# One bank and two written-out orders of a convolution and SiLU kernel on one core

## The chip, the cores and the metric

The kernel runs on one core of a Trainium2 chip. The metric is the device time of one execution in microseconds (us); the time before is the median of three runs. A separate profiled execution gives the trace.

## What is computed

```python
B, S, D = x.shape                       # 8, 4096, 192
w = softmax(weight, axis=-1)            # 8 heads x 7 taps
x_pad = zeros(6 rows) + x               # per sequence
out[b, s, h, g] = sum_k w[h, k] * x_pad[b, s + k, h, g]
h = out.reshape(32768, 192) @ w_in      # 192 x 2048
result = (h * sigmoid(h)) @ w_out       # 2048 x 192
```

A causal convolution of seven taps per head, then an up projection, SiLU, and a down projection, all in fp32.

## The kernel before, in words

**Blocks.** The 32,768 rows are cut into 32 blocks of 1,024 rows, each held as two halves of 512. Channels lie on partitions; 64 input channels are one contraction, so two products can lie on the two halves of the array's rows (`e` = 0 uses partitions 0 to 63, `e` = 1 partitions 64 to 127). From block 1 on both projections are computed with fewer multiplications, by sums of inputs and of weights.

**Up phase.** For five groups g of chunks (order `QUEUE`: 0, 4, 1, 2, 3) there are 15 products P*r*.*g* each (line 625), in three chains, each of which accumulates in a PSUM bank of its own: chain 1 is P5, P2, P6, P1, P0, P14, chain 2 is P3, P9, P7, P4, P8, chain 3 is P12, P10. Between two products of chain 1 ScalarE (ACT) copies the bank (tokens u5, u4, u2, u0, u1, line 674); between two of chain 2 VectorE (DVE) adds bank and copy (X2, X4 into the banks 5 and 6, then a5, a1, a0 into the hidden activations, line 668); after P12 and P10 VectorE subtracts bank 4 (b1, b5). P13 and P11 add to the banks 5 and 6. S0 to S5 are SiLU on ScalarE (line 686). `CHAIN_BANKS` names the bank of each chain and group; chain 3 has bank 4 in every group. One chunk is left plain: L.nk (line 642) is the product of half n with input part k. L.0k fills bank `PLAIN_BANKS[0]`; L.1k is two products of 256 columns, one on each half of the rows, into `PLAIN_BANKS[1]` and `PLAIN_BANKS[2]`. SL.0, SL.1 and SL.2 are their SiLUs (line 691).

**Down phase.** t.ji (line 709) are differences of hidden activations on VectorE. D*i*.*je* (line 741) are 48 groups of four products, 32 columns of the array each; i = 5 has 128 columns, the others 512. They add up in the banks `ACC` = 7, 1, 3, 5, 6, 4 for i = 0 to 5. z, y, x (lines 807, 804, 799) copy these banks on ScalarE, M1 to M7 (line 819) add them on VectorE, o transposes (line 829) and st stores them.

**Input of the next blocks.** ld loads two blocks ahead, i transposes on VectorE (line 464), ha sets the halo, v.ki is tap i of the convolution of part k (i = 0 on ScalarE, line 495, the rest on VectorE, line 498), sp spreads the result by DMA to both halves of the partitions (line 515), w makes sums of it (lines 532 and 535).

**The order.** Everything is issued in the order of two written-out lists of such tokens. `START` covers the first blocks (dp are the down products of block 0), `PLAN` is then run once per block; "-", "=" and "+" ahead of a token mean one block back, two back, one ahead. Engines work through their own instructions in that order, and `pin` keeps it. Each slot between two bars of `PLAN` holds one token of TensorE, so the list can be read as TensorE's order with the other engines' work beside it: "P12.1 | P6.2 u1.1 a5.1" puts u1.1 and a5.1 behind P6.2. Tiles and banks are reused, and a writer waits for the readers before it: P9 for X2, P10 for b1, P2 for u5, L.1k for whatever last read its banks.

```python
    QUEUE = (0, 4, 1, 2, 3)
    CHAIN_BANKS = ((0, 1, 7, 1, 0), (2, 3, 2, 3, 2), (4, 4, 4, 4, 4))
    CHAINS = ((5, 2, 6, 1, 0, 14), (3, 9, 7, 4, 8), (12, 10))
    ACC = (7, 1, 3, 5, 6, 4, 0)
    PLAIN_BANKS = (7, 7, 3)
    for b in range(3, NB + 2):
        for s in plan:
            for t in s:
                step(b, t)
```

Of the kernel before, what the change touches and what calls it, by code (L numbers as in the profile page):

```python
# [17 lines left out]
def kernel(  # L18
# [60 lines left out]


    PLAN = (
        "P5.0 | -P8.3 -S3.2 -sp.2 v.00 -t.01 | -D1.31 -S2.3 -S5.2 | -D1.01 -a0.2 -S1.3 =st.2 "
        "-a0.3 -S1.1 | -D1.11 -b5.3 -S0.2 | -D0.00 -S5.4 v.22 -sp.0 -S4.3 | -D2.01 -t.03 "
        "-S5.1 -S1.2 | -D0.20 =st.0 -t.02 -S0.3 | -D1.21 -S5.3 v.01 | -D2.00 v.11 | -D5.01 "
        "+ld.0 | -D0.30 v.02 | -D3.00 -t.10 | -D0.01 +ld.1 v.23 | -D0.31 v.24 | -D4.00 -t.11 "
        "+ld.2 | -D3.01 -w.0 | -D4.01 | -D0.11 -t.13 | -D2.11 -w.1 | -D5.00 | -D4.11 -t.12 | "
        "-D5.11 | -D2.10 -t.20 | -D4.10 -t.21 | -D5.10 | -D0.21 | -D0.10 -t.23 | -D3.11 "
        "-z1.0 v.25 u5.0 | -D4.20 v.03 | -D1.10 -t.22 | -D3.10 | -D4.21 -t.30 | -D1.20 v.12 "
        "| -D2.20 -t.31 | -D2.21 | -D1.30 -t.32 | -D3.21 -t.33 | -D5.20 | -D2.31 v.04 | "
        "-D1.00 v.26 | -D4.31 -w.2 | -D2.30 v.05 | -D5.30 -y2.0 | -D3.20 v.06 -y1.0 -M1.0 | "  # L90
        "-D3.31 v.13 | -D3.30 -M2.0 | -D5.31 v.14 -x0.0 | -D4.30 -y0.0 -M3.0 | -D5.21 -x1.0 "
        "| P2.0 | L.00 -M4.0 -x2.1 -w.3 | L.01 | P5.4 u4.0 -w.4 | L.02 | P6.0 u5.4 v.15 | "
        "P3.0 | P2.4 SL.0 v.16 u2.0 | L.12 -x2.3 X2.0 | L.11 -x2.2 u4.4 | L.10 -M5.0 | P9.0 "
        "| P1.0 +i.0 SL.2 SL.1 | P13.0 | P6.4 +i.1 -x2.0 u0.0 X4.0 | P3.4 | P5.1 u2.4 +i.2 "
        "S2.0 | P7.0 | P0.0 -M6.0 +ha.0 X2.4 | P12.0 | P11.0 u1.0 a5.0 u5.1 | P9.4 | P1.4 "
        "b1.0 S4.0 | P13.4 | P4.0 u0.4 X4.4 -w.5 | P10.0 | P2.1 a1.0 | P0.4 | P7.4 u4.1 b5.0 "
        "S2.4 | P11.4 | P8.0 -o.1 u1.4 a5.4 | P6.1 | P12.4 S4.4 a0.0 | P14.4 | P14.0 -M7.0 "
        "u2.1 S0.0 b1.4 | P4.4 | P3.1 S3.4 +v.10 | P10.4 | P1.1 X2.1 S3.0 a1.4 | P5.2 | P9.1 "
        "u0.1 | P0.1 | P13.1 u5.2 X4.1 | P2.2 b5.4 | P8.4 -o.3 | P7.1 | P5.3 u4.2 a0.4 -st.3 "
        "u1.1 | P6.2 | P12.1 S2.1 a5.1 u5.3 | P11.1 | P3.2 -st.1 b1.1 u2.2 S5.0 | P4.1 | "  # L100
        "P10.1 X2.2 S4.1 sp.1 | P2.3 S1.0 | P9.2 a1.1 -o.0 | P1.2 | P8.1 u4.3 X4.2 | P6.3 | "
        "P13.2 u0.2 a0.1 +v.20 | P11.2 b5.1 | P7.2 u2.3 -o.2 S2.2 | P0.2 | P3.3 S4.2 a5.2 | "
        "P1.3 | P12.2 u1.2 X2.3 | P4.2 u0.3 | P9.3 b1.2 S0.4 | P14.1 | P10.2 S1.4 X4.3 | "
        "P0.3 S3.1 | P7.3 b5.2 | P11.3 u1.3 a1.2 | P12.3 S0.1 a5.3 | P14.3 | P13.3 +v.21 | "
        "P4.3 S3.3 b1.3 | P8.2 a1.3 | P10.3 | P14.2 t.00"
    )
    START = (
        "=dp.37 =v.20 =v.00 =dp.19 =v.10 =dp.5 =dp.10 =dp.42 =dp.36 =dp.27 =dp.44 =dp.14 "
        "=dp.8 =dp.12 =dp.38 =dp.28 =dp.22 =dp.25 =dp.43 =dp.26 =dp.45 -ld.2 =dp.30 =dp.3 "
        "=dp.20 -ld.1 =dp.33 =dp.11 -ld.0 =dp.6 =v.01 =dp.17 =v.21 =dp.15 =v.02 =dp.18 =v.11 "  # L110
        "=v.03 =dp.16 =v.12 =dp.47 =v.04 =dp.0 =v.22 =v.13 =dp.23 =v.05 =dp.32 =v.14 =dp.34 "
        "=v.06 =dp.7 =v.15 =sp.0 =v.23 =dp.21 =v.16 =dp.4 =v.24 =sp.1 =dp.40 =v.25 =dp.39 "
        "=v.26 =go.2 =dp.31 -i.2 =sp.2 =dp.1 -i.1 -i.0 =dp.9 -ha.0 =dp.13 =dp.46 =dp.35 =w.0 "
        "-v.20 =dp.41 -v.10 =w.1 =dp.2 -v.11 =w.2 -L.01 -P5.0 -v.21 -L.00 -P5.4 -u5.0 =w.3 "
        "-L.02 -P2.0 -v.22 -v.12 =dp.24 -u4.0 -v.23 -v.00 =dp.29 -SL.0 =w.5 -u5.4 -P6.0 -P3.0 "
        "=cp.1 =cp.2 -P2.4 -u2.0 -X2.0 -L.12 -u4.4 -L.10 -v.01 =cp.0 -L.11 -P9.0 -P1.0 =o.0 "
        "-SL.2 -P13.0 -P6.4 -u0.0 -X4.0 -v.13 -P3.4 -P0.0 -u2.4 =w.4 -S2.0 -P12.0 -P11.0 "
        "-SL.1 -X2.4 -u1.0 -P7.0 -P5.1 -S4.0 -b1.0 -P9.4 -P1.4 -a5.0 -u5.1 -v.14 -P4.0 -P10.0 "
        "-u0.4 -X4.4 -P0.4 -a1.0 -v.15 -P2.1 -P7.4 -b5.0 -P8.0 -P11.4 -u4.1 -a5.4 -u1.4 -v.02 "
        "-P6.1 -P13.4 -a0.0 -P12.4 -P14.0 -u2.1 -v.03 -S2.4 -P3.1 -P1.1 -b1.4 -S3.0 -P4.4 "  # L120
        "-P14.4 -X2.1 -u0.1 -v.04 -P0.1 -P9.1 -S3.4 -a1.4 -S4.4 -P10.4 -P5.3 -X4.1 -P8.4 "
        "-v.16 -P5.2 -u5.3 -b5.4 -P7.1 -P2.3 -a0.4 -u5.2 -sp.1 -P12.1 -S5.0 -a5.1 -P2.2 -u1.1 "
        "-P13.1 -P4.1 -b1.1 -u4.2 -P3.2 =o.2 ld.2 -S2.1 -P6.2 -u4.3 -a1.1 -P10.1 -v.05 -P11.1 "
        "-u2.2 -P8.1 -X2.2 -P6.3 +ld.1 -S4.1 -v.24 -S0.4 -P9.2 -P1.2 -u2.3 -b5.1 -P14.1 "
        "-P13.2 -X4.2 -u0.2 ld.1 -a0.1 -P1.3 -P7.2 -S2.2 -v.25 -S3.1 -P0.2 -P3.3 -u0.3 -a5.2 "
        "-S1.0 =st.2 -P12.2 -P0.3 -X2.3 -u1.2 -P11.2 -P9.3 -b1.2 -u1.3 =st.0 -v.26 -P10.2 "
        "-P4.2 -S4.2 -X4.3 -P13.3 -P14.3 ld.0 -b5.2 -P14.2 -P7.3 -a1.2 -S2.3 -S1.4 -P12.3 "
        "-P11.3 -a5.3 -S0.0 -S3.3 -P4.3 -P8.2 -b1.3 -S0.1 =o.1 -S3.2 P5.0 -P10.3 -v.06 -S1.2 "
        "-D1.31 -t.00 u5.0 -sp.0 -S5.1 -D1.11 -a1.3 -D1.10 -t.01 =st.1 -D0.11 i.1 -sp.2 "
        "-D1.00 -a0.2 i.0 -S0.2 -D1.30 -t.03 -S5.2 -D0.00 -S4.3 -S1.3 -b5.3 -D2.00 -S1.1 "  # L130
# [12 lines left out]
        "a5.4 S4.4 P5.2 P3.1 b1.4 u2.1 P4.4 P10.4 u5.2 X2.1 v.16 P2.2 P9.1 a1.4 sp.1 P1.1 "
        "P13.1 u4.2 b5.4 X4.1 P8.4 P6.2 u0.1 +i.1 S1.0 P7.1 P0.1 a0.4 u2.2 S2.1 +i.0 P2.3 "
        "P12.1 u1.1 a5.1 +ha.0 P3.2 P1.2 b1.1 P4.1 u0.2 X2.2 P10.1 u4.3 P11.1 a1.1 P9.2 S0.4 "
        "-M7.0 P6.3 S4.1 P8.1 b5.1 P0.2 u2.3 P13.2 X4.2 +v.20 a0.1 P7.2 P11.2 u1.2 -o.0 S2.2 "
        "P3.3 P1.3 S0.1 a5.2 S4.2 P14.1 P12.2 X2.3 +v.10 u0.3 P9.3 P4.2 b1.2 P10.2 P0.3 X4.3 "
        "P11.3 P7.3 u1.3 b5.2 S0.0 a1.2 P12.3 P14.3 S5.0 a5.3 S1.4 P13.3 -o.2 S3.1 P4.3 b1.3 "
        "S3.3 P8.2 P14.2 a1.3 P10.3 t.00 +v.21"
    )  # L150
    QUEUE = (0, 4, 1, 2, 3)
    CHAIN_BANKS = ((0, 1, 7, 1, 0), (2, 3, 2, 3, 2), (4, 4, 4, 4, 4))

    def pin(ins):
        return tc.keep_in_program_order(ins)
# [37 lines left out]
    x0 = x.flatten_outer_dims()[TB - pad : TB, :].rearrange("t (k c) -> c k t", k=NK)  # L193
# [357 lines left out]
    def rows(t, e):  # L551
        return t[R * e : R * e + R]
# [46 lines left out]
    X_OF = {13: 0, 10: 5, 5: 3, 11: 4, 14: 1}  # L599
    CHAINS = ((5, 2, 6, 1, 0, 14), (3, 9, 7, 4, 8), (12, 10))  # L600
    ACC = (7, 1, 3, 5, 6, 4, 0)
    PLAIN_BANKS = (7, 7, 3)
    XBANK = {2: 5, 4: 6}

    def chain_bank(g, c):
        return banks[CHAIN_BANKS[c][QUEUE.index(g)]]

# [27 lines left out]
    def plain(b, n, k):  # L635
# [3 lines left out]
        for e in range(2) if n else (0,):  # L639
            cols = slice(e * TB // 2, (e + 1) * TB // 2) if n else slice(0, TB)  # L640
            pin(
                nc.tensor.matmul(  # L642
                    banks[PLAIN_BANKS[n and 1 + e]][:, cols],
                    rows(wr[j] if own == e else ws[j], e)[:, a, k, :],
# [7 lines left out]
    def h_of(b, g, o):  # L652
        a, j, e = PLAIN if g is None else chunks(g)[o // 2]
        return g_tile(b, j, a)[:, o % 2, e, :]
# [33 lines left out]
    def silu_plain(b, i):  # L688
        cols = slice((i - 1) * TB // 2, i * TB // 2) if i else slice(0, TB)
        h = h_of(b, None, int(i > 0))[:, cols]  # L690
        pin(nc.scalar.activation(h, banks[PLAIN_BANKS[i]][:, cols], AF.Silu))

# [418 lines left out]
```

## Time and profile before

| | |
|---|---|
| median of three runs | 2359.14 us (2359.13 to 2359.39) |
| profiled execution | 2359.21 us |
| its span, first to last instruction | 2357.4 us |
| granted TensorE clock | 0.999 |
| one block in the middle of the run, start of D to start of D | 72.38 us |
| DVE busy in the 36.10 us of its D phase | 32.86 us |
| DVE busy in the 36.20 us of its P phase | 32.68 us |
| ACT busy in the two phases | 9.39 us, 27.40 us |

The span is the time from the first to the last recorded instruction; the execution's own time has some 1.8 us around it. PE is TensorE's matmuls, PEld its weight loads, which run ahead of the matmuls and wait in their place. A row of the list of waits reads: who waited, for whom, in total us, how often, the longest. A matmul's end is modelled, so that two matmuls which follow each other with a short delay still count as one busy stretch.

### The profile page before, as it was taken

To read this page: it belongs to the slowest core of one execution; us is meant where nothing else is said; L and a number is where in the kernel's file an instruction comes from. 1 tells how busy PE (TensorE), PEld (TensorE's weight loads), DVE (VectorE), ACT (ScalarE), POOL (GpSimd) and SP (SyncE) were. 2 spreads that over 40 slices of the span, in tenths; PEclk is the share of its full clock that TensorE was granted. 3 is DMA by queue.
4 is the path that set the end of the run, shared out by engine and by line. 5 is a ranking of instruction groups with operands and counts; after the bars stand their busy time and mean duration, and the time that the engine had idled before them with its cause. 6 is when DMAs were issued, how large, how long until landed. Compare 5 with 4: busy or idle time off the path is not lost.

```text
span 2357.4 us, 43991 instructions
## 1 busy us (share of the span) xinstructions
PE 2349.2 (100%) x17630; PEld 1043.8 (44%) x17630; DVE 2110.6 (90%) x2877; ACT 1179.4 (50%) x2275; POOL 105.7 (4%) x168
## 2 busy tenths in 40 slices
PE   9999999999999999999999999999999999999998
PEld 4344443444444444444444444444444444444444
DVE  8999989899899999998998999999999989899867
ACT  5345644456544465444564445654446644456443
POOL 4910000000000000000000000000000000000000
PEclk9999999999999999999999999999999999999999
DMA  7232111222112221222221122212222112222111
GB/s 158 51 66 52 37 35 35 52 53 47 26 33 52 53 53 29 38 40 52 53 43 28 35 53 52 52 23 36 48 52 52 36 32 37 52 53 39 21 20 28
DMA packets 451245, 106.56 MB, mean 45 GB/s; under 512 B 423584, under 2 KB 428704, under 8 KB 451040
## 3 DMA queue, kind: packets, MB, share of 16 engines
q1 hardware_dynamic: 447392, 101.78, 23.7%
q8 instruction: 138, 2.26, 0.4%
q0 software_dynamic: 448, 1.58, 0.3%
q10 hardware_dynamic: 3200, 0.39, 0.1%
q14 instruction: 67, 0.55, 0.1%
HBM read 31.46 MB, written 25.17 MB: 24 GB/s over the span
## 4 chain that ended last, share of the span: by engine, by line
PE 99%; DVE 1%; ACT 0%; issue 0%; ACTq 0%; DVEq 0%
PE ps L741 47%; PE ps L625 45%; PE ps L642 2%; PE ps L762 2%; PE ps L570 2%; PE ps L1010 1%; PE ps L422 0%; DVE t L709 0%; DVE g L668 0%; DVE cmb L819 0%; DVE cmb L162 0%; ACT u L162 0%; ACT yx L804 0%; DVE osb L162 0%; DVE win L532 0%
## 5 line engine op out<-in xcount | busy, mean ns | idle before, releaser
L741 PE MATMUL ps<-g,wo 128*32 128x512 f32 x2976 | 691.9, 592 | 0.0
L625 PE MATMUL ps<-win,wr 64*128 64x512 f32 x1550 | 691.3, 595 | 0.0
L625 PE MATMUL ps<-win,ws 64*128 64x512 f32 x1550 | 674.3, 603 | 0.6 <-ACT u L674 0.6
L674 ACT COPY u<-ps 128x512 f32<-128x512 f32 x775 | 445.8, 589 | 184.6 <-PE ps L625 158.0
L741 PE MATMUL ps<-t,wo 128*32 128x512 f32 (+2 forms) x4528 | 536.6, 446 | 0.5 <-DVE t L709 0.5
L741 PE MATMUL ps<-t,wx 128*32 128x512 f32 x2976 | 495.7, 592 | 0.0
L625 PE MATMUL ps<-dup,wr 64*128 64x512 f32 x868 | 423.8, 590 | 0.0
L498 DVE SCALAR_TENSOR_TENSOR nat<-xt,taps,nat 128x512 f32<-128x512 f32 x564 | 415.4, 755 | 5.6 <-ACT nat L495 2.0
L709 DVE TENSOR_TENSOR t<-g 128x1024 f32<-128x1024 f32 x248 | 299.9, 1220 | 61.1 <-PE ps L741 41.0
L709 DVE TENSOR_TENSOR t<-g,t 128x1024 f32<-128x1024 f32 x248 | 302.7, 1221 | 30.0 <-PE ps L741 24.7
L625 PEld LDWEIGHTS ps<-win,wr 64*128 64x128 f32 x1550 | 261.4, 186 | 148.3 <-issue 62.4
L686 ACT ACTIVATE g<-ps 128x512 f32<-128x512 f32 x465 | 275.4, 602 | 83.8 <-PE ps L625 78.0
L668 DVE TENSOR_TENSOR g<-u,ps 128x512 f32<-128x512 f32 x465 | 305.7, 673 | 10.1 <-PE ps L625 1.4
L741 PEld LDWEIGHTS ps<-t,wo 128*32 128x32 f32 x4528 | 185.4, 110 | 274.2 <-issue 270.6
L625 PEld LDWEIGHTS ps<-win,ws 64*128 64x128 f32 x1550 | 242.6, 185 | 144.8 <-issue 49.5
L625 PE MATMUL ps<-dup,ws 64*128 64x512 f32 x682 | 280.9, 602 | 0.0
L668 DVE TENSOR_TENSOR ps<-u,ps 128x512 f32<-128x512 f32 x310 | 214.5, 692 | 69.8 <-PE ps L625 64.0
L686 ACT ACTIVATE g<-g 128x512 f32<-128x512 f32 x465 | 268.4, 633 | 15.3 <-DVE g L668 15.3
L804 ACT COPY yx<-ps 32x512 f32<-32x512 f32 x150 | 84.2, 579 | 380.0 <-PE ps L741 377.6
L741 PE MATMUL ps<-g,wx 128*32 128x512 f32 x1488 | 246.0, 594 | 0.0
L741 PEld LDWEIGHTS ps<-g,wo 128*32 128x32 f32 x2976 | 170.1, 110 | 112.5 <-issue 103.9
L807 ACT COPY cmb<-ps 96x512 f32<-96x512 f32 x30 | 17.5, 583 | 403.8 <-PE ps L741 403.8
(90 smaller groups left out, 1849.2 us busy)
## 6 DMA issues: line engine op xcount, KB each, us to landing
dup<-nat SPq DMA_DIRECT2D x345, 128.0 KB, 2.3
nat<-in_x_dram SPq DMA_DIRECT2D x382, 64.0 KB, 2.4
out_dram<-osb SPq DMA_DIRECT2D x376, 64.0 KB, 2.0
raw<-in_moe_w_out_dram SPq DMA_DIRECT2D x8, 384.0 KB, 3.6
raw<-in_moe_w_in_dram SPq DMA_DIRECT2D x12, 192.0 KB, 4.5
ws<-wr POOLq DMA_DIRECT2D x8, 192.0 KB, 5.0
raw<-in_moe_w_in_dram SPq DMA_DIRECT2D x6, 128.0 KB, 3.0
xt<-xt SPq DMA_DIRECT2D x31, 4.5 KB, 1.9
```

What stands on the lines that cost most here:

```text
L498: nc.vector.scalar_tensor_tensor(out=dst, in0=src, scalar=tap, in1=dst, op0=ALU.mult, op1=ALU.add)
L570: nc.tensor.matmul(hs[a, n, e], rows(wr[j], e)[:, a, k, :], rows(d, e)[:, n, k, :], start=k == 0, stop=k == NK - 1,)
L625: nc.tensor.matmul(to[:, cols], raw(g, *LEFT[e][r], e), rhs[:, cols], start=first, stop=True, skip_group_check=True,)
L642: nc.tensor.matmul(banks[PLAIN_BANKS[n and 1 + e]][:, cols], rows(wr[j] if own == e else ws[j], e)[:, a, k, :], rows(dups[b], e)[:, SLOT[e ...
L668: pin(nc.vector.tensor_tensor(out_, u, v, op=op))
L674: pin(nc.scalar.copy(us[b, g, o][:, cols], t1[:, cols]))
L686: pin(nc.scalar.activation(h, src, AF.Silu))
L709: pin(nc.vector.tensor_tensor(t[i // 2][:, i % 2, :], u, v, op=ALU.subtract))
L741: nc.tensor.matmul(accs[b][at][SQ * q : SQ * q + SQ, to], lhs[:, e, SQ * k : SQ * k + SQ], rhs[:, e, ts(q, TB // 4) if i == 5 else to], st ...
L762: nc.tensor.matmul(banks[DOWN_BANKS[k]][R * n : R * n + R, :], wo[j][:, a, e, R * k : R * k + R], gs[b, j, a][:, n, e, :], start=j == 0 an ...
L804: pin(nc.scalar.copy(to, acc[3 * (name[0] == "x") + k][n:P, :]))
L1010: nc.tensor.matmul(by_pe[k][n], rows(diag, n)[:, k, i, :], rows(xts[0], n)[:, k, i : i + TB], start=i == 0, stop=i == K - 1,)
```

## The change

`PLAIN_BANKS` goes from (7, 7, 3) to (7, 4, 3), and moves up beside the other tables: the first 256 columns of L.1k now lie in bank 4, which is that of chain 3, instead of bank 7, which holds L.0k. Both lists are written anew with the same tokens. Of the tokens of `PLAN`, nine have another block sign, since they stand at the other end of the list now (v.00, v.21, sp.0, st.0, st.2, a0.2, S0.1, S1.1, S5.1). In the diff, lines that are only "..." mark what is left out; the new `PLAN` is whole.

```diff
     PLAN = (
-        "P5.0 | -P8.3 -S3.2 -sp.2 v.00 -t.01 | -D1.31 -S2.3 -S5.2 | -D1.01 -a0.2 -S1.3 =st.2 "
...
-        "S2.0 | P7.0 | P0.0 -M6.0 +ha.0 X2.4 | P12.0 | P11.0 u1.0 a5.0 u5.1 | P9.4 | P1.4 "
-        "b1.0 S4.0 | P13.4 | P4.0 u0.4 X4.4 -w.5 | P10.0 | P2.1 a1.0 | P0.4 | P7.4 u4.1 b5.0 "
...
-        "P0.3 S3.1 | P7.3 b5.2 | P11.3 u1.3 a1.2 | P12.3 S0.1 a5.3 | P14.3 | P13.3 +v.21 | "
-        "P4.3 S3.3 b1.3 | P8.2 a1.3 | P10.3 | P14.2 t.00"
+        "P5.0 | -P8.3 -S0.1 -t.01 -S3.2 | -D0.11 -S5.2 v.01 -S2.3 | -D0.10 -a0.3 -S1.3 +ld.0 "
+        "-t.02 | -D1.20 -S0.3 -S5.4 | -D2.00 -S1.2 -t.03 -S4.3 | -D0.00 +ld.1 v.21 | -D2.01 "
+        "-b5.3 | -D1.21 v.22 -S5.3 -sp.2 | -D4.01 -S0.2 -t.10 | -D1.01 -t.11 | -D4.00 | "
+        "-D3.01 -t.12 | -D3.00 -t.13 +ld.2 | -D5.00 | -D2.11 -w.0 | -D5.01 | -D0.01 v.11 | "
+        "-D0.30 -t.20 | -D4.11 v.12 | -D4.10 v.02 | -D5.10 | -D2.10 -t.21 | -D3.10 -t.23 | "
+        "-D1.10 | -D5.11 v.13 | -D1.11 -w.1 | -D5.20 | -D1.00 v.03 | -D3.11 v.23 | -D1.30 "
+        "v.04 -t.22 | -D0.31 | -D4.21 -t.30 | -D1.31 -w.2 | -D0.20 v.14 | -D4.20 -t.31 | "
+        "-D2.21 | -D2.20 | -D5.21 -t.33 | -D2.31 | -D3.20 -t.32 | -D0.21 v.15 | -D5.30 -z1.0 "
+        "| -D2.30 v.05 | -D5.31 -M1.0 | -D3.31 -x2.2 v.24 -y2.0 | -D3.21 -x2.3 -w.3 u5.0 | "
+        "-D4.31 -x2.0 v.06 | -D3.30 v.25 | -D4.30 -w.5 -x0.0 -y1.0 -M2.0 | P3.0 | P2.0 -y0.0 "
+        "-M3.0 -x2.1 | P5.4 | L.01 -w.4 u4.0 -M4.0 | L.11 u5.4 +i.0 | P6.0 | L.00 -x1.0 v.16 "
+        "| L.10 u2.0 | P2.4 | L.02 X2.0 | L.12 -M5.0 u4.4 | P1.0 | P9.0 -o.1 SL.2 SL.0 | "
+        "P6.4 | P13.0 v.26 SL.1 u0.0 X4.0 | P5.1 | P3.4 u2.4 +i.2 S2.0 | P0.0 | P7.0 X2.4 | "
+        "P1.4 | P12.0 u1.0 a5.0 | P11.0 | P9.4 b1.0 u0.4 -M6.0 | P4.0 | P13.4 S4.0 u5.1 X4.4 "
+        "| P0.4 | P10.0 a1.0 | P7.4 | P2.1 u1.4 b5.0 | P11.4 | P8.0 S5.0 a5.4 u4.1 -M7.0 | "
+        "P14.0 | P14.4 S2.4 a0.0 | P12.4 | P6.1 S3.4 +i.1 S3.0 | P3.1 | P4.4 +ha.0 b1.4 u2.1 "
+        "| P5.2 | P10.4 X2.1 a1.4 | P1.1 | P9.1 u5.2 -o.2 S4.4 | P2.2 | P8.4 u0.1 -st.2 X4.1 "
+        "| P5.3 | P13.1 b5.4 u4.2 -o.3 | P7.1 | P0.1 u5.3 a0.4 S2.1 | P12.1 | P6.2 u1.1 a5.1 "
+        "S0.0 | P2.3 | P3.2 b1.1 u2.2 S1.0 | P4.1 | P10.1 X2.2 u4.3 | P11.1 | P9.2 a1.1 b5.1 "
+        "| P1.2 | P8.1 S4.1 -o.0 | P6.3 | P12.2 u0.2 X4.2 -st.0 a0.1 | P0.2 | P13.2 u2.3 "
+        "t.00 | P1.3 | P3.3 -st.1 S2.2 u1.2 | P11.2 | P7.2 X2.3 sp.1 | P14.2 b1.2 S4.2 | "
+        "P9.3 a5.2 u0.3 | P14.1 | P10.2 +v.10 X4.3 S5.1 | P0.3 -st.3 S0.4 | P7.3 b5.2 | P4.2 "
+        "u1.3 | P12.3 S1.4 a5.3 | P14.3 +v.20 a1.2 | P13.3 | P4.3 b1.3 S3.3 | P8.2 sp.0 "
+        "+v.00 | P11.3 a1.3 S1.1 | P10.3 a0.2 S3.1"
     )
     START = (
-        "=dp.37 =v.20 =v.00 =dp.19 =v.10 =dp.5 =dp.10 =dp.42 =dp.36 =dp.27 =dp.44 =dp.14 "
...
-        "S3.3 P8.2 P14.2 a1.3 P10.3 t.00 +v.21"
+        "=dp.41 =v.00 =v.20 =dp.14 =v.10 =dp.22 =dp.37 =dp.0 =dp.23 =dp.44 =dp.43 =dp.26 "
...
+        "-v.02 =dp.5 =w.3 =dp.36 -v.12 -v.03 =cp.1 -P2.0 -L.00 =cp.0 -P3.0 -P5.4 -u4.0 =cp.2 "
+        "-L.10 -u5.4 -P6.0 =o.2 -v.21 -L.11 -u2.0 -L.02 -P2.4 -X2.0 -L.12 =w.4 -u4.4 -P1.0 "
+        "-P13.0 -SL.0 =w.5 -SL.1 -P6.4 -P9.0 -u0.0 -v.04 -SL.2 -P0.0 -P12.0 -u2.4 -X4.0 -v.22 "
...
+        "-P6.2 -v.15 -P7.1 -S2.1 -b1.1 -P11.1 -P3.2 -u2.2 -a5.1 -S1.4 -P1.2 -P10.1 -u5.3 "
+        "-X2.2 -P4.1 -v.23 -u0.2 -P9.2 -S4.1 -a1.1 -P13.2 -P0.2 -X4.2 -P8.1 -P2.3 -u1.2 -b5.1 "
+        "-S5.4 -v.16 -P11.2 -P7.2 -u4.3 -a0.1 -sp.1 -S2.2 -P14.2 -P12.2 -v.05 -P3.3 -P6.3 "
+        "-S3.2 -b1.2 -t.00 -D1.00 -u2.3 =st.0 -S4.2 -D1.31 -v.24 -X2.3 -D1.20 =st.1 -v.06 "
+        "-D1.21 -a5.2 +ld.1 -t.01 -P1.3 -P9.3 -P10.2 -P14.1 -u0.3 -X4.3 -S1.1 -P4.2 -P13.3 "
+        "ld.0 -b5.2 -S0.1 -P0.3 -P7.3 -a1.2 -P12.3 -P11.3 -u1.3 -a5.3 =st.2 -S5.2 -P14.3 "
...
+        "P4.3 b1.3 +v.10 P13.3 P14.2 +v.20 a1.3 P10.3 +v.00 t.00 S0.4 sp.0 a0.2 -st.2"
     )
     QUEUE = (0, 4, 1, 2, 3)
     CHAIN_BANKS = ((0, 1, 7, 1, 0), (2, 3, 2, 3, 2), (4, 4, 4, 4, 4))
+    PLAIN_BANKS = (7, 4, 3)
...
     ACC = (7, 1, 3, 5, 6, 4, 0)
-    PLAIN_BANKS = (7, 7, 3)
```

## The prediction

> **What bounds the kernel now.** I read the page first, then the list of waits, then the windows and the timeline of one block in the middle of the run, because the page alone looks finished:
>
> ```profile
> span 2357.4 us, 43991 instructions
> PE 2349.2 (100%) x17630; PEld 1043.8 (44%) x17630; DVE 2110.6 (90%) x2877; ACT 1179.4 (50%) x2275; POOL 105.7 (4%) x168
> PE 99%; DVE 1%; ACT 0%; issue 0%; ACTq 0%; DVEq 0%
> ```
>
> TensorE is never idle in the records, so its own stretches must hold the loss. The windows cut one block at its two phases: the up products (P, L), then the down products (D).
>
> ```profile
> 1264.90:1301.10 36.20, 36.20 (x176) 20.03 (x168) 32.68 (x52) 27.40 (x54) 0.62 (x1) 1.00 0.17 33
> 1228.80:1264.90 36.10, 36.10 (x385) 12.04 (x384) 32.86 (x39) 9.39 (x18) 0.00 (x0) 1.00 0.30 52
> ```
>
> (Columns: length; busy PE, PEld, DVE, ACT, POOL; clock; DMA share; GB/s.) In the timeline a product is two passes whose starts are 0.429 us apart when nothing is late (0.214 for half columns). A P product uses 64 rows, so two run side by side: call e=0 lane 0, e=1 lane 1. Per block each lane has 39 full and three half-width products: 39 x 0.858 + 3 x 0.429 = 34.75 us. The phase runs from 1264.97 to 1301.04 (last pass of P8.3 at 1300.61 plus 0.43), 36.07: lane 0 loses 1.32. The D phase has 40 x 0.858 + 8 x 0.215 = 36.04 in 36.1: nothing to win there. Two excerpts of the timeline show what a loss looks like (start, duration):
>
> ```profile
> 1267.66 1.14 PE L625 MATMUL ps<-win,wr 64*128 64x512 f32 x4
> 1267.92 0.60 ACT L691 ACTIVATE g<-ps 128x512 f32<-128x512 f32 x1 [0.29 <-PE ps L625]
> 1268.57 0.18 PEld L642 LDWEIGHTS ps<-dup,ws 64*128 64x128 f32 x1 [0.59 <-ACT g L691]
> ...
> 1280.27 1.02 PE L625 MATMUL ps<-win,wr 64*128 64x512 f32 x4
> ...
> 1281.44 0.70 DVE L668 TENSOR_TENSOR ps<-u,ps 128x512 f32<-128x512 f32 x1 [0.59 <-PE ps L625]
> ...
> 1282.19 0.69 PE L625 MATMUL ps<-win,ws 64*128 64x512 f32 x1
> ...
> 1282.72 0.83 PE L625 MATMUL ps<-win,ws 64*128 64x512 f32 x2
> ```
>
> First: L.12 writes bank 7 in its first half and must wait until SL.0 has read L.0x from it; SL.0 starts at 1267.92, L.12 at 1268.57. Second: P3.1's second pass starts at 1280.70, its sum X2.1 on VectorE 0.74 later, P9.1 on the same bank 0.75 after that, its second pass 0.53 later instead of 0.43. So a product that waits for a DVE sum needs 1.45 us after the second pass of its forerunner, and late ones pay 0.105 more. Two pairs further in a lane is only 0.429 + 0.858 = 1.287: 0.16 late, with the second pass 0.26. For an ACT copy (u) the same sum is about 1.31: 0.02 late, some 0.08 to 0.10 lost (P0.3, u1.3, P14.3). The list of waits says that this is in every block:
>
> ```profile
> PEld ps L625 <- ACT u L674: 53.0, 154, 1.4
> PEld ps L625 <- DVE ps L668: 42.5, 123, 0.8
> PEld ps L625 <- DVE u L668: 32.9, 88, 0.6
> PEld ps L642 <- ACT g L691: 17.9, 30, 0.7
> ```
>
> Those are idle times of the weight loader, which runs ahead; the price in matmul starts is what I add up. Lane 0 in this block: entry after D 0.10; L.12 0.05 + 0.105; P9.1 0.21 + 0.105; P10.1 0.15 + 0.105; P9.3 0.16 + 0.105; P7.3 0.09 + 0.105. Sum 1.29 of the 1.32. Lane 1 loses about 1.2 (many u copies at 0.08; then P14.2, queued behind P10.3, which waits for b1.3 behind the conv step v.21: 0.30 + 0.105), so lane 0 sets the end.
>
> **What the Trainium skill says.** "TensorE: Matmul & The Clock Gate", section The mechanism: tiles on different row groups overlap; the trace agrees, with the two lanes' starts 0.01 us apart (1264.97, 1264.98). "PSUM — Partial Sum Buffer", section PSUM bank collisions raise a hardware error: accesses are to be guarded by bank and quadrant; that is the L.12 wait, 0.65 us from SL.0's start. "Perfetto Trace Analysis", section Tensor Engine Instruction: the end of a matmul is estimated, so I use starts alone. Same page, Matmuls: independent groups should rotate through banks so that reading one overlaps the next; the new bank does this for L.1.
>
> **The change, part by part.** No instruction is added or removed; the orders and one bank differ.
>
> 1. Bank of L.1's first half, 7 to 4, and the order of the plain chunk. L.12's wait for SL.0 goes: 0.155 of lane 0. L.1 now waits for the copies x2.0 to x2.3 of the last block's D5 sums. In the new list ACT does x0.0, y1.0, y0.0, x2.1. x0.0 starts 1.11 us after D3.30 (1263.82 against 1262.71 in the block above), and D3.30 is now second to last, 1.72 before the end of D: -0.61. Such copies follow each other by 0.49 (y0.0 at 1264.31), so y1.0, y0.0 and x2.1 start at -0.12, +0.37 and +0.86. L.01 (bank 7, behind y0.0) comes at +0.115 switch + 0.533 + 0.429 = +1.08; y0.0 lets go at +1.02 (0.65 after its start). In time by 0.06; I put 0.03 for a late second pass. L.11 at +1.9 has x2.1 0.7 earlier. P12.0, next on bank 4, stands well after SL.1.
>
> 2. Pairs that are too close, counted in the new list. DVE: P12.4-b1.4-P10.4, P3.1-X2.1-P9.1, P12.1-b1.1-P10.1, P3.2-X2.2-P9.2, P4.1-a1.1-P8.1, P3.3-X2.3-P9.3, P9.3-X4.3-P7.3, P10.2-b5.2-P12.3, P4.2-a1.2-P8.2, P4.3-a1.3-P8.3: ten; the old list has nine. What counts is how many stalls cover them, since a stall of 0.26 between the two ends of another pair, in the same lane, gives that one its 0.16. Old: P9.1, P10.1 (covers P9.2, P8.1), P9.3 (covers P10.2), P7.3 (covers P12.3): four, as the trace has it. New: P10.4 (covers P9.1), P10.1, P9.3, P7.3: four again, at 0.26, 0.26, 0.26, 0.20 = 0.98 against 1.03. P8.2 has 0.1 us in hand behind a5.3 and a1.2.
>
> 3. ACT pairs too close: seven in the old list (P6.0, P2.4, P0.1, P2.2, P6.2, P6.3, P14.3), four in the new (P2.2, P0.2, P1.3, P14.3); and v.21 no longer stands before b1.3. All in lane 1, which falls to about 0.6: worth nothing, as lane 0 ends last.
>
> New lane 0: 0.10 + 0.03 + 0.98 = 1.11 against 1.29: 0.18 us a block. If P10.4 does not cover P9.1, 0.26 more (a loss of 0.08); if L.01 is in time entirely, 0.03 less.
>
> 4. The D phase and queues. First D's: D0.11 behind S3.1 on ACT, D0.10 behind S0.1, D1.20 behind S3.2; also with v.00 now on ACT before them these are due 0.4 us or more ahead of their D. The t sums are over 1.2 us early, as before (their D's wait nowhere). SP: sp.0 moves before the end of the P phase and waits there for P13.3 and P14.3; queued behind it are the loads ld.0, ld.1 and sp.2. w.0 needs sp.2 and comes about six D's (5 us) later; landing takes 2.3. The stores are spread through the P phase, before the t tile that takes their buffer. POOL: halo copy only. All hidden; a transfer late by a D would cost 0.86 a block.
>
> 5. The first blocks. The down products of block 0 and P of block 1 are mixed otherwise, D of block 1 starts four at a time before P of block 1 ends. In before, the P of block 1 takes 104.3 to 139.66, 35.3 for a nominal 32.2: 3.1 lost, mostly to VectorE, which has 28.6 us of work listed inside 31.3 us of products besides a backlog of convs. New: 24.2 in 27.5 and 5.2 in 6.0, D's between. I estimate 1 us won there, one extra switch D-P-D (0.3) paid: -0.7, bounds -4 to +3. The last block's end is the same code.
>
> Sum: 29 P phases (blocks 3 to 31) x 0.18 = 5.2, plus 0.7: 5.9 us. The profiled run is 2359.21 us with a span of 2357.4, 0.07 above the median of 2359.14; 2359.2 - 5.9 = 2353.3.
>
> **Rivals.** (a) No change that can be measured, where 0.2% (4.7 us) is what can: P9.1 still stalls behind P10.4, or the lag that lane 0 sheds early returns at P9.3 and P7.3, since these depend on VectorE. 0.18 - 0.26 + part of it: -1 to +1 us, 2358 to 2360. For it: DVE is 90% busy in both phases. Against: X2.1 gets 1.55 us in my sum where 1.45 are needed. (b) Slower: L.01 behind y0.0. Both lanes come behind it in queue order through L.11. It decides from 0.15 us later than I have it (0.1 stall plus 0.105 takes the 0.18); at 0.4 later it costs 0.34 + 0.105 - 0.03 - 0.18 = 0.24 a block, +7 us: 2366. For it: only 0.06 us in hand and a queue of three copies behind x0.0, which waits for D3.30. Against: their times are measured. (c) The first blocks turn bad: SL.1, SL.2, cp.0 crowd bank 4 while VectorE is behind; +3 with the steady gain kept: 2357. (d) The gain is larger: no late second passes, P8.2 and P10.1 covered by lane 1's ease, first blocks -4: 2348.
>
> **Chances.** Forecast (2350 to 2354.5) 0.40, (d) 0.13, (a) and (c) together 0.27, (b) and other losses 0.20. Faster by over 0.2% 0.53, within 0.27, slower 0.20. The range takes (d), (a), (c) and the low part of (b): 2347 to 2362.
>
> **What would show it.** Blocks 72.2 us apart instead of 72.38 (D start to D start in the timeline); the line PEld L642 behind ACT L691 nearly gone; PEld L625 behind ACT u much lower; a stall at P10.4 and none at P9.1; P7.3 still 0.09 to 0.16 late. I am wrong if PEld waits at L642 behind ACT yx L804 in every block, if D products wait for t or S, or if blocks take 72.4.

## The result: 8.6 us slower

The changed kernel takes 2367.80 us (median of 6 runs, 2367.17 to 2368.01), the kernel before in the same runs 2359.18 us: a ratio of 1.0036, 95% interval 1.0023 to 1.0049. Its profiled span is 2366.2 us, 8.8 more than before. The two pieces below are the page's head and its chain of work:

```profile
span 2366.2 us, 43941 instructions
PE 2354.3 (100%) x17630; PEld 1129.7 (48%) x17630; DVE 2100.2 (89%) x2877; ACT 1186.4 (50%) x2275; POOL 101.8 (4%) x168
...
PE 96%; ACT 2%; DVE 1%; SPq 0%; issue 0%; DMA 0%; ACTq 0%; DVEq 0%
```

TensorE still looks full; that 2% of the chain is now ScalarE, where it was 0%, is the one hint on the page. In the trace the blocks, D start to D start, are 72.734 us apart (median of 29) instead of 72.375. The windows of one block, cut at its phases, say which half grew (length; busy PE, PEld, DVE, ACT, POOL; clock; DMA share; GB/s):

```profile
1232.70:1268.90 36.20, 36.20 (x385) 12.04 (x384) 32.00 (x39) 7.91 (x18) 0.44 (x1) 1.00 0.22 42
1268.90:1305.50 36.60, 36.48 (x176) 23.11 (x172) 33.34 (x51) 29.28 (x56) 0.00 (x0) 1.00 0.24 44
```

The down phase is as long as it was. The up phase went from 36.16 to 36.52 us (from its first matmul to the next block's first D), and 0.12 us of its window has no matmul at all, which was not so before. The span adds up: the first D of block 2 comes at 214.10 instead of 215.51 us (-1.41); 29 blocks at +0.36 give +10.4, and one of them, the fourth, is another 0.35 longer; from the last of these D's to the end it is 42.39 instead of 43.04 (-0.65). Together +8.7 of the 8.8.

The list of waits names the new wait:

```profile
ACT yx L804 <- PE ps L741: 38.3, 30, 1.4
...
DVE cmb L819 <- ACT yx L804: 29.1, 29, 2.8
...
PEld ps L625 <- DVE cmb L819: 27.4, 29, 0.9
...
PEld ps L625 <- ACT u L674: 24.7, 96, 1.2
```

The two lines with 29 events are one wait per steady block: VectorE's sums (L819) behind ScalarE's copies (L804), and a weight load of a P product behind these sums. The first stood in the list before as well, with 88 waits, three a block and 0.34 us each on average; the second has no counterpart there. The line "PEld ps L642 <- ACT g L691", L.12 behind SL.0, is gone as predicted, and the waits behind ACT u fell from 53.0 to 24.7 us. The timeline of the end of a D phase shows the new wait at work (start, duration, engine; the last bracket is idle time and what ended it):

```profile
1268.27 1.78 ACT L804 COPY yx<-ps 32x512 f32<-32x512 f32 x3 [1.27 <-PE ps L741]
1268.42 0.61 PE L741 MATMUL ps<-t,wx 128*32 128x512 f32 x3
...
1268.96 1.13 PE L625 MATMUL ps<-win,wr 64*128 64x512 f32 x4
1269.47 1.28 DVE L819 TENSOR_TENSOR cmb<-cmb,ps 96x512 f32<-96x512 f32 x2 [0.94 <-ACT yx L804]
...
1270.20 0.18 PEld L625 LDWEIGHTS ps<-dup,wr 64*128 64x128 f32 x1 [0.94 <-DVE cmb L819]
1270.21 0.69 PE L625 MATMUL ps<-dup,wr 64*128 64x512 f32 x1
1270.28 0.18 PEld L642 LDWEIGHTS ps<-dup,ws 64*128 64x128 f32 x1
1270.31 0.67 PE L642 MATMUL ps<-dup,ws 64*128 64x512 f32 x1
```

Read it from the bottom. L.01 (L642) starts at 1270.31, P5.4 (the L625 of 1270.21) just ahead of it; from the phase's start at 1268.96 both were due at +0.96, 1269.92. P5.4 is the first writer of bank 1. That is D1's bank, which M2.0 on VectorE reads; M2.0 starts at 1269.47 after 0.94 us of nothing. It waits for y1.0, which reads the same bank on ScalarE, and y1.0 is the second of the three copies in the first row, behind x0.0, which waits for D3.30, second to last D. Before, y1.0 stood ahead of the last D's, and M2.0 started 2.07 us ahead of the phase.

### The profile page after: what moved, and what is told of

The parts are those of the page before. It is cut to its first block, busy times and chain, and to the rows that moved or that the text cites. A ratio compares the mean times of both kernels' runs of the same rounds, so it can differ in the third digit from the quotient of the medians.

```text
span 2366.2 us, 43941 instructions
## 1 busy us (share of the span) xinstructions
PE 2354.3 (100%) x17630; PEld 1129.7 (48%) x17630; DVE 2100.2 (89%) x2877; ACT 1186.4 (50%) x2275; POOL 101.8 (4%) x168
## 4 chain that ended last, share of the span: by engine, by line
PE 96%; ACT 2%; DVE 1%; SPq 0%; issue 0%; DMA 0%; ACTq 0%; DVEq 0%
PE ps L741 46%; PE ps L625 44%; PE ps L642 2%; PE ps L762 2%; PE ps L571 2%; ACT yx L804 2%; DVE cmb L819 1%; PE ps L1010 1%; SPq L838 0%; PE ps L423 0%; SPq L181 0%; DMA nat<-in_x_dram 0%; DVE cmb L163 0%; ACT u L163 0%; ACT g L686 0%
## 5 line engine op out<-in xcount | busy, mean ns | idle before, releaser
L741 PE MATMUL ps<-g,wo 128*32 128x512 f32 x2976 | 711.3, 593 | 0.0
L625 PE MATMUL ps<-win,ws 64*128 64x512 f32 x1550 | 652.4, 596 | 0.4 <-ACT u L674 0.4
L625 PE MATMUL ps<-win,wr 64*128 64x512 f32 x1550 | 642.2, 597 | 0.0
L741 PE MATMUL ps<-t,wo 128*32 128x128 f32 (+2 forms) x4528 | 555.2, 446 | 0.0
L625 PE MATMUL ps<-dup,wr 64*128 64x512 f32 x868 | 411.5, 593 | 3.4
L668 DVE TENSOR_TENSOR g<-u,ps 128x512 f32<-128x512 f32 x465 | 310.6, 679 | 22.8 <-PE ps L625 17.8
L625 PEld LDWEIGHTS ps<-win,wr 64*128 64x128 f32 x1550 | 253.5, 186 | 156.4 <-issue 57.0
L625 PE MATMUL ps<-dup,ws 64*128 64x512 f32 x682 | 307.2, 606 | 0.0
L686 ACT ACTIVATE g<-g 128x512 f32<-128x512 f32 x465 | 278.9, 628 | 54.4 <-DVE g L668 54.4
L625 PEld LDWEIGHTS ps<-win,ws 64*128 64x128 f32 x1550 | 253.3, 186 | 97.1 <-DVE ps L668 28.4
L741 PE MATMUL ps<-g,wx 128*32 128x512 f32 x1488 | 255.4, 592 | 0.0
L668 DVE TENSOR_TENSOR ps<-u,ps 128x512 f32<-128x512 f32 x310 | 214.2, 691 | 39.4 <-PE ps L625 28.7
L741 PEld LDWEIGHTS ps<-t,wx 128*32 128x32 f32 x2976 | 120.4, 110 | 226.5 <-issue 223.3
```

Source lines behind the costliest of these rows:

```text
L625: nc.tensor.matmul(to[:, cols], raw(g, *LEFT[e][r], e), rhs[:, cols], start=first, stop=True, skip_group_check=True,)
L668: pin(nc.vector.tensor_tensor(out_, u, v, op=op))
L686: pin(nc.scalar.activation(h, src, AF.Silu))
L741: nc.tensor.matmul(accs[b][at][SQ * q : SQ * q + SQ, to], lhs[:, e, SQ * k : SQ * k + SQ], rhs[:, e, ts(q, TB // 4) if i == 5 else to], st ...
```

## Experiments

Theory A: the loss is P5.4 <- M2.0 <- y1.0 <- x0.0 <- D3.30. Theory B, which the prediction had as a rival: L.01 waits for y0.0 by itself. All edits start from the changed kernel's `PLAN` unless said otherwise; times are medians, ratios those to the kernel before in the same runs.

**1. y1.0 early.**

```diff
-... -y2.0 | ... -x0.0 -y1.0 -M2.0 | P3.0 | P2.0 -y0.0
+... -y2.0 -y1.0 | ... -x0.0 -M2.0 | P3.0 | P2.0 -y0.0
```

> The changed kernel with one token moved: ScalarE's copy y1.0 one place earlier, right behind y2.0, so that it no longer waits behind x0.0 for the last chunks of D3. Theory A (P5.4 waits for VectorE's product M2.0, which waits for y1.0's read of the same bank): M2.0 starts when D3's last chunk lets it, P5.4 is on time, and y0.0 too moves forward by a copy: the group of waits of the weight loads at L625 behind VectorE's combine at L819 goes, a block takes some 0.40 us less, 2355 us (2353 to 2358). Theory B (only L.01 is late, it waits for y0.0's read of bank 7): y0.0 is not behind x0.0 by more than before, the gain is at most that of one copy, with the wait at L642 shrinking and not that at L625; 2360 to 2364 us. Neither: 2367 us.

2352.91 us, 0.9973 (0.9963 to 0.9983): 14.9 us less than the changed kernel, faster than both, and 0.1 below A's range. Blocks are 72.237 apart. Of its list of waits:

```profile
ACT yx L804 <- PE ps L741: 16.9, 30, 1.4
...
ACT yx L804 <- DVE cmb L819: 9.0, 29, 0.3
...
PEld ps L642 <- ACT yx L804: 6.8, 29, 0.2
...
DVE cmb L819 <- ACT yx L804: 1.6, 1, 1.6
```

The sums no longer wait for copies, but for one event, and the line of L625 behind L819 is gone. Two things went at once, though: in its timeline y0.0 follows x0.0 directly, and L.01 (L642) starts at +0.96, on time.

```profile
1260.63 1.06 ACT L804 COPY yx<-ps 32x512 f32<-32x512 f32 x2 [0.53 <-PE ps L741]
...
1261.35 1.13 PE L625 MATMUL ps<-win,wr 64*128 64x512 f32 x4
...
1262.31 0.59 PE L642 MATMUL ps<-dup,ws 64*128 64x512 f32 x1
```

The next three runs separate the two.

**2. y0.0 early, y1.0 as it was.**

```diff
-... -x0.0 -y1.0 -M2.0 | P3.0 | P2.0 -y0.0
+... -y0.0 -x0.0 -y1.0 -M2.0 | P3.0 | P2.0
```

> The changed kernel with one token moved: ScalarE's copy y0.0 ahead of x0.0 and y1.0; y1.0 and M2.0 stay at the end. Theory A: L.01 is free early, but P5.4 ahead of it in the written order still waits for M2.0 behind y1.0 and L.01 stands behind P5.4: hardly any gain, or a loss if y1.0 is now a copy later (2366 to 2370 us). Theory B: the wait was L.01's own for y0.0; it goes, 2356 us (2354 to 2359).

2367.59 us, 1.0035 (1.0022 to 1.0048), 72.740 a block: nothing gained, as A said. L.01 is free, but starts with P5.4, which stands ahead of it and is late, at +1.25 instead of +0.96. So A's wait alone costs all of the 0.50 us by which a block is longer than in run 1.

**3. M2.0 early.**

```diff
-... -M1.0 | ... -y1.0 -M2.0 |
+... -M1.0 -M2.0 | ... -y1.0 |
```

> The changed kernel with one token moved: VectorE's product M2.0 right behind M1.0, ahead of ScalarE's y1.0, so that the read of y1.0 comes after it and no longer holds P5.4's bank longer than before. Theory A: P5.4's stall of 0.38 us shrinks or becomes y1.0's own read; if y1.0 too must be done before P5.4, its end (0.6 us before y0.0's) is in time, and only L.01's wait for y0.0 of 0.2 to 0.3 us is left: 0.1 to 0.2 us a block less, 2361 to 2364 us. Theory B: no gain, 2367 us.

2360.76 us, 1.0006 (0.9997 to 1.0014), 0.2 below A's range, 72.498 a block. Its timeline, phase start 1265.96:

```profile
1265.23 1.78 ACT L804 COPY yx<-ps 32x512 f32<-32x512 f32 x3 [1.25 <-PE ps L741]
...
1266.92 0.59 PE L625 MATMUL ps<-dup,wr 64*128 64x512 f32 x1
...
1267.07 0.69 PE L642 MATMUL ps<-dup,ws 64*128 64x512 f32 x1
...
1267.78 0.59 PE L642 MATMUL ps<-dup,wr 64*128 64x256 f32 x2
...
1268.04 0.38 PE L642 MATMUL ps<-dup,ws 64*128 64x256 f32 x1
```

The copies stand where they stood; P5.4 is on time (+0.96), and L.01 alone is late, by 0.157, with 0.104 more for its second pass: what y0.0 itself costs. So taking A's wait away gains 0.236 of the 0.50 us a block between the changed kernel and run 1, and y0.0 keeps the other 0.26. The two waits overlap: A's alone costs the whole (run 2), y0.0's alone about half. B was not wrong, it lay hidden under A. Lane 1 stays on time here: the last two rows are the two halves of L.11, that of lane 1 first.

**4. y1.0 and M2.0 later still, y0.0 early.**

```diff
-... -x0.0 -y1.0 -M2.0 | P3.0 | P2.0 -y0.0 -M3.0
+... -x0.0 | P3.0 | P2.0 -y0.0 -y1.0 -M2.0 -M3.0
```

> The changed kernel with y0.0 between x0.0 and y1.0, and M2.0 behind y1.0: y0.0 is early (x0.0 and y0.0 write the same partitions and should start 0.49 us apart), y1.0 and M2.0 come about 0.49 us later. Theory A (P5.4 waits for M2.0): P5.4 0.49 us later still, 14 us more, 2382 us (2378 to 2385). Theory B (L.01 waits for y0.0 alone): 0.2 to 0.4 us a block less, 2356 to 2361 us.

2381.43 us, 1.0093 (1.0077 to 1.0108), 0.6 from A's number; B's sign is wrong. The 0.48 us that y1.0 is later comes back in every block: 73.212 against 72.734.

```profile
1274.56 1.65 ACT L804 COPY yx<-ps 32x512 f32<-32x512 f32 x3 [1.27 <-PE ps L741]
...
1276.25 1.28 DVE L819 TENSOR_TENSOR cmb<-cmb,ps 96x512 f32<-96x512 f32 x2 [1.43 <-ACT yx L804]
1276.98 0.18 PEld L625 LDWEIGHTS ps<-dup,wr 64*128 64x128 f32 x1 [1.43 <-DVE cmb L819]
```

VectorE's and the weight loader's wait went from 0.94 to 1.43 together.

**5. The bank alone, in the lists of before.** The changed lists can't keep the old bank: L.0k and L.1k alternate in them, and would mix in bank 7. The lists of before can take the new one, if the x2 copies are moved ahead of L.1k, which now writes the bank that they read. In `START`, cp.0 and SL.1 move a few places for the same reason.

```diff
-    PLAIN_BANKS = (7, 7, 3)
+    PLAIN_BANKS = (7, 4, 3)
-... -x2.1 ... u4.0 ... SL.0 ... L.12 -x2.3 ... L.11 -x2.2 ... -x2.0
+... -x2.1 -x2.3 -x2.2 -x2.0 ... u4.0 ... SL.0 ... L.12 ... L.11 ...
```

> The kernel before with the bank of the plain chunk's L.1 parts changed alone (the third chain's bank), its lists kept but for the four x2 copies of D5, which are moved ahead together so that the bank is read out before L.1 writes it, and two tokens in the first blocks' list. Theory A: the wait of L.12 for ScalarE's SL.0 (0.155 us a block) goes and nothing of P5.4 comes, since y1.0 stands ahead of the last D chunks: 2354 to 2356 us. If the bank change itself costs (theory C: the loss is the bank's and not the lists'), 2362 us or more.

2372.31 us, 1.0055 (1.0042 to 1.0068). No test of the bank: four copies in a row put u4.0 off, P6.0 behind it was 0.43 us late, and every block 0.37 longer. The second form puts the copies into ScalarE's gaps:

```diff
+... -x2.1 -x2.3 ... u4.0 -x2.2 ... u5.4 -x2.0 ... SL.0 ... L.12 ...
```

> Again the kernel before with the bank of L.1 alone changed, now with the x2 copies put into gaps of ScalarE (x2.3 behind x2.1, x2.2 behind u4.0, x2.0 behind u5.4), so that u4.0 and with it P6.0 are not pushed back as they were when all four stood together (P6.0 0.43 us late). Theory A: L.12's stall of 0.155 us goes and nothing comes in its place: 0.13 to 0.18 us a block less, 2354.5 us (2353 to 2357). Theory C (the bank change itself is what costs): 2362 us or more.

2360.68 us, 1.0006 (0.9998 to 1.0014): neither expectation. L.12's stall is gone, yet a block is 72.338, only 0.04 shorter, four of the 29 are 0.1 to 0.4 longer than the others, and the first blocks cost 1.5 us. The bank costs nothing by itself, so theory C, that it is the bank which costs, falls; but the stall that it removes was not worth 0.155 here. In before, lane 1 was 0.13 us late at this place too (P6.0 0.08, P2.4 0.05, both behind u copies). In this run lane 0 leads lane 1 through the plain chunk by just that, L.12 starting 0.13 ahead in the upper row (L643 is L642 here and L669 is L668, by one line more in the lists):

```profile
1270.49 0.38 PE L643 MATMUL ps<-dup,ws 64*128 64x256 f32 x1
...
1270.61 0.38 PE L643 MATMUL ps<-dup,wr 64*128 64x256 f32 x1
...
1271.00 0.70 DVE L669 TENSOR_TENSOR ps<-u,ps 128x512 f32<-128x512 f32 x1
```

Two other waits take the gain back. The last row is X2.0, behind u2.0 and SL.0: from the phase's start it comes 0.02 later than before, while P9.0, which waits for it, is due 0.15 sooner. P9.0's second pass is 0.083 late, and the lead shrinks to 0.05. Then P9.1 waits 0.25 us for X2.1 instead of 0.21. X2.1 reads what P3.1 of lane 0 wrote, but it starts 0.74 us after the second pass of P4.4, which stands ahead of P3.1 in the list and in lane 1: so it is in before and in both forms of this run, while its distance from P3.1's own second pass is 0.75, 1.14 and 0.79. So lane 1 holds lane 0 back there. That raised the question whether lane 0 can lead at all.

**6. A stall in lane 1 alone.** From run 1, with u5.4 later, so that P2.4 in lane 1 is late and nothing in lane 0 waits.

```diff
-| L.01 -w.4 u4.0 -M4.0 | L.11 u5.4 +i.0 | P6.0 | L.00 -x1.0 v.16
+| L.01 -w.4 u4.0 -M4.0 | L.11 +i.0 | P6.0 | L.00 -x1.0 u5.4 v.16
```

> The version with y1.0 early (2352.9 us), with ScalarE's u5.4 one place later, behind x1.0, so that P2.4 in lane 1 alone is late by about 0.29 us and 0.105 for its second pass, where lane 0 has no wait; lane 1 loses 0.5 us less than lane 0 over the block. If a lane's own losses count alone, as the prediction had it, the block is as long as before: 2352 to 2354 us. If a lane can't run ahead of the other, the loss is passed to lane 0 and the block is 0.3 to 0.4 us longer: 2362 to 2365 us. In between if lane 0 keeps part of its lead.

2354.29 us, 0.9979 (0.9970 to 0.9987), 0.3 above the first expectation, and no answer. The dose was missed: x1.0 had waited for u5.4 and moved up, u5.4 was on time but for 0.03 us, seen in P2.4's second pass. But L.02, next to it in lane 0, was 0.04 late as well, and the block is 72.283, longer by 0.046. So once more with u5.4 behind u2.0:

> As the run before, with u5.4 behind u2.0 instead, because behind x1.0 it made P2.4 only 0.03 us late (u5.4 started at 41.25 us of the block, not 41.6). Now u5.4 starts at about 42.2 us and P2.4, in lane 1, comes at 42.85 instead of 41.96: 0.89 us late and 0.105 for its second pass. Lane 1 has about 0.55 us in hand at the end of the block. If a lane's own losses count alone, 0.45 us a block are lost: 2366 us (2364 to 2368). If lane 0, whose L.02 stands behind P2.4 in the list, is held up with it, about 1.0 us a block: 2381 us (2378 to 2384).

2381.86 us, 1.0096 (1.0082 to 1.0110); 73.242 a block, 1.005 more than run 1.

```profile
1278.46 1.07 ACT L674 COPY u<-ps 128x512 f32<-128x512 f32 x2 [0.50 <-PE ps L625]
...
1279.58 0.18 PEld L625 LDWEIGHTS ps<-win,wr 64*128 64x128 f32 x1 [1.13 <-ACT u L674]
1279.59 0.69 PE L625 MATMUL ps<-win,wr 64*128 64x512 f32 x1 [0.73 <-ACT u L674]
...
1279.59 0.69 PE L642 MATMUL ps<-dup,ws 64*128 64x512 f32 x1
```

The L642 of the last row is L.02, in lane 0: its bank is free, its inputs are there, its list place is behind P2.4, and it starts with it. The whole delay is passed on; what lane 1 has in hand at the block's end saves nothing.

Not every wait is passed on. In the first form of run 5, P6.0 in lane 1 starts 0.43 us late; P3.0, behind it in lane 0, is due only 0.43 us after that start, and is on time. In run 3 L.01 in lane 0 is late, and P6.0 and P1.0 in lane 1 start as in run 1. In these runs a product that waits holds what stands behind it in the list, in both lanes, but the other lane loses only what goes beyond the time at which its next product is due. In this run that product, L.02, was due at once.

The Trainium skill ("PSUM — Partial Sum Buffer", section Engine vs sequencer instructions) has it that matmuls start and complete in program order. L.02 behind P2.4 agrees, and X2.1, which waits for P4.4, agrees for the completion. The starts do not keep to it throughout: in run 3 the half of L.11 in lane 1 starts 0.25 us ahead of the half in lane 0, which the kernel issues first.

**7. Wider pairs.** From run 1, to test the prediction's price of a pair: P12.4 ahead of P14.4, so that P10.4 is three products behind P12.4.

```diff
-| P14.0 | P14.4 S2.4 a0.0 | P12.4 | P6.1 S3.4 +i.1 S3.0 | P3.1 |
+| P14.0 | P12.4 S2.4 a0.0 | P14.4 | P6.1 +i.1 S3.0 S3.4 | P3.1 |
```

> The version with y1.0 early (2352.9 us), and P14.4 and P12.4 swapped, with S3.4 behind S3.0: in lane 0 the order is P12.4, P14.4, P3.1, P10.4, P9.1, so that P10.4 stands three products behind P12.4 instead of two, and only P9.1 two behind P3.1. If a pair two apart costs 0.26 us and one three apart nothing, as the prediction's second step has it, P10.4's 0.26 and P9.1's 0.18 become one stall of 0.26 at P9.1: 0.18 us a block less, 2347.7 us (2346.5 to 2350). Rival: lane 1 or VectorE's queue takes it back (VectorE is 89% busy), 2351 to 2354 us.

2357.54 us, 0.9993 (0.9985 to 1.0001), 72.408 a block: not the gain, and worse than the rival. Its timeline shows a slip of the edit:

```profile
1279.25 0.58 ACT L674 COPY u<-ps 128x512 f32<-128x512 f32 x1
...
1279.86 0.70 DVE L668 TENSOR_TENSOR ps<-u,ps 128x512 f32<-128x512 f32 x1 [0.60 <-ACT u L674]
```

X2.1 also needs u2.1, which S3.4 had pushed back; it waited for that copy and P9.1 for X2.1. The next run keeps u2.1 ahead of S3.4 and puts P1.1 and P0.1 ahead of P5.2 and P2.2:

> The version with y1.0 early (2352.9 us), with P12.4 ahead of P14.4 once more, now with P1.1 and P0.1 ahead of P5.2 and P2.2, so that ScalarE's u2.1, which the sum X2.1 also needs, stays ahead of S3.4 and on time (in the run before it had been put back to 54.24 us of the block, and X2.1 with it by 0.15 us). If a pair three products apart costs nothing, the two stalls at P10.4 and P9.1 (their starts 0.26 us late in sum) are one of 0.24 to 0.26 us still: P9.1 alone is late, and the block is as long as before, 2352 to 2354 us, because P10.4's stall had covered P9.1's already; if instead both stalls counted, 0.18 us a block less, 2347.7 us. If lane 1, which is now rewritten, ends last, more than 2354 us.

2363.80 us, 1.0019 (1.0011 to 1.0028). P10.4's wait is down to 0.03, P9.1's to 0.03, each still with a second pass late by 0.104; P8.4, the next in lane 0, starts 54.19 us after the block's first D, to the hundredth as in run 1. So the two stalls do cover each other, the first of the three expectations, though both are late a little instead of P9.1 alone. The loss of 0.36 a block comes after it: the edit put P5.3 one place back in lane 1, so its copy u5.3 starts 1.08 us later; S2.1, S0.0 and u2.2 queue behind it on ScalarE, u2.2 ends 0.49 later, X2.2 waits for u2.2, and P9.2 is 0.27 late, with more second passes on the way.

## Why the prediction was wrong

It gave 2353.3 us and a range of 2347 to 2362, as faster. **The step that failed is the first**, at its sentence that y0.0 is "in time by 0.06", for which 0.03 us was put. Two terms were wrong in it:

- *A wait not counted.* It followed the copies only to L.01. P5.4 stands one place ahead, and its bank is read by M2.0 behind y1.0. Alone this costs 0.50 us a block, the whole loss (run 2 against run 1); with y0.0 late as well, taking it away gains 0.236 (run 3). The way to it was in the old list of waits and timeline:

```profile
DVE cmb L819 <- ACT yx L804: 29.7, 88, 3.0
...
1262.90 0.68 DVE L819 TENSOR_TENSOR cmb<-cmb,ps 96x512 f32<-96x512 f32 x1
...
1263.82 1.67 ACT L804 COPY yx<-ps 32x512 f32<-32x512 f32 x3 [1.61 <-PE ps L741]
```

In three places of every block a sum starts 0.03 us after the end of a copy that reads the same bank: M1.0 behind y2.0, M3.0 behind x0.0, M4.0 behind x1.0. M2.0 (1262.90) was not one of them: it ran 0.7 us after y1.0, behind a convolution step, and two microseconds ahead of the phase. The Trainium skill's section that the prediction names ("PSUM — Partial Sum Buffer", PSUM bank collisions raise a hardware error) counts reads of one bank by ScalarE and VectorE as collisions, though not in different quadrants of 32 rows. Here M2.0 reads rows 0 to 95 and y1.0 rows 96 to 127, and the kernel orders them all the same. Whether they could run together was not tried.
- *A size.* "Such copies follow each other by 0.49" was read from one pair, x0.0 to y0.0. The next pair in the same row, y0.0 to x1.0, is 0.60 apart. With y1.0 between, the pitches are 0.59 to 0.61, so y0.0 is at +0.62 after the end of D and not +0.37, and L.01 0.157 + 0.104 late (run 3).

Counted from the starts of passes as the prediction does it, lane 0 loses 1.31 us in a block before, 1.68 in the changed kernel and 1.18 in run 1. L.01 (0.39 + 0.08) and P9.0 (0.04) are what the changed kernel has more than run 1.

With y1.0 moved back, run 1 takes 2352.91 us: what the prediction said for the whole change. Part of that is luck: its 29 steps from block to block save 3.65 us and not 5.2, the first blocks and the end together 2.7 and not 0.7. The other terms, by their steps:

1. L.12's wait behind SL.0 went, as said. In run 1 lane 0 loses nothing in the plain chunk; in the lists of before the same was worth 0.04 and not 0.155, since P9.0 and P9.1 come later there (run 5).
2. Right: P10.4 stalls (0.15 + 0.104) and covers P9.1; in run 1 P10.1 loses 0.254, P9.3 0.266, and P7.3 0.264 and not 0.20. With 0.104 at entry these make 1.14 us of lane 0's 1.18, against 1.11 predicted. The prediction's 1.31 us behind a u copy, 0.02 too late, is a little long: P14.3's first pass is on time in before, and its second alone is 0.08 late.
3. Right in run 1: lane 0 ends last. It loses 0.13 us less than before, the block is 0.14 shorter, where 0.18 was predicted, and that lane 1 loses 0.40 instead of 1.09 adds nothing to be seen. As a rule it is too simple, since lane 1 can hold lane 0 through its place in the list (run 6, and X2.1 in run 5).
4. Right: the D phase is as long as before, 36.22 us. Weight loads of D wait for S, 22.5 us in all, but less than before (39.4), and no D is late for it.
5. In the bounds: -1.41 us by block 2, -0.7 predicted; the end, "the same code", gave another -0.65, and the fourth block 0.35 back. What makes that block longer stays open.

Rival (b) came within 2 us of the time, 2366, and had the right queue of copies behind x0.0. But its sign, a wait at L642 behind L804, is not in the list: P5.4 waits first, and L.01 behind it in the queue shows no wait for a copy. In run 1, the fastest, that line stands with 29 waits, and L.01 is on time: weight loads run ahead, and their wait alone is no loss. Its odds were set from 0.06 us in hand, which rested on one measured pitch.

## What to carry to other kernels

Where a reader is moved towards a phase's end, follow every bank that it holds, through other engines' reads of the same bank, to the first writer, and start with the writer that stands first in TensorE's order, for all others queue behind it. Overlapping row groups share that order: a wait in one holds what stands behind it in the other, and delays it by what goes beyond the time at which it is due. Of two waits that coincide, removing one gains less than it costs alone: nothing in run 2, 0.236 of 0.50 in run 3. After a hand edit of an order, look at what each moved instruction pushed back; four of the ten edits here were decided by that.

## What was not expected of the hardware

**ScalarE copies overlapped only where their first rows match.** x0.0 and y0.0 both read rows 96 to 127 and write rows 0 to 31: the second starts 0.49 us after the first, 0.09 before its end, in before, run 1 and run 4. Copies that write other rows than the one ahead (x0.0 to y1.0, y1.0 to y0.0, y0.0 to x2.1) start 0.01 to 0.03 after its end, 0.59 to 0.61 apart: 1.78 us for three in the changed kernel, 1.65 in run 4, which has one such change less. Likewise y2.0 and x2.3, same rows, overlap by 0.09, while x2.3 to x2.2 and x2.3 to u5.0 do not; and z1.0 (rows 0 to 95) and u5.0 (all rows), which start at the same row and end at different ones, overlap by 0.10 in before. The Trainium skill ("ScalarE: Activation LUTs", section What ACT_TABLE_LOAD costs) gives 93 ns of overlap for instructions back to back, which is the matching case. That the first row of input or output is what decides is read from the pairs of these orders, and no run was made for it alone; run 4 predicted one pair, 0.49, and got 0.49.

**A wait costs more than its length, and a release just in time costs too.** A P product that waited for its bank pays about 0.104 us at its second pass, also where the wait was 0.03 us (P10.4 and P9.1 in run 7's second form). In one block each of before, the changed kernel and run 1 the second pass of these comes 1.27 to 1.29 us after the start of the VectorE sum ahead of it, or 1.16 to 1.17 after that of the ScalarE copy, however long the wait was. The same distances hold where the first pass was on time and the second alone was late: P9.0 in run 5 (1.28 behind X2.0, 0.083 late) and P14.3 in before (1.17 behind u1.3, 0.081 late).
